# Q and K of 128 later rows computed during the weight load, kept in DRAM, and read back in steps 16 to 19, with a new order and ungated last loads

## The chip, the cores and the metric

The kernel runs on one core of one Trainium2 chip. The metric is device time in microseconds, the median of the runs shown. Before the change it is 2654.93 us (three runs, 2654.26 to 2665.12).

## The reference

A transformer of two layers with one set of weights, over 2048 rows `x` of width 576, bfloat16. Each layer is a memory-augmented attention and a gated feed-forward, both on a layer norm of the residual stream:

```python
for s in range(n_seg):                       # 64 segments of 32 rows
    xs = x[:, s * seg_len:(s + 1) * seg_len, :]
    h = concatenate([mem, xs], axis=1)       # 8 memory rows + 32 rows
    q, k, v = h @ Wq, h @ Wk, h @ Wv         # 32 heads of 128
    p = softmax(where(mask, q @ k.T * scale, -1e9))
    o = (p @ v) @ Wo
    mem = o[:, :M, :]                        # memory of the next segment
    outs.append(o[:, M:, :])
...
x = x + A(layernorm(x)); x = x + B(layernorm(x))     # B: (silu(x w1) * (x w3)) w2, F = 4608
x = x + A(layernorm(x)); x = x + B(layernorm(x))
```

The memory makes the segments a chain: segment s+1 needs the eight memory rows that segment s puts out. Q and K of the 32 rows of a segment don't need the memory.

## The kernel before

**Steps.** The two layers run interleaved. In step t, layer 0 treats segment t and layer 1 segment t - 8 (`LAG`, line 32), so there are 72 steps. Steps 0 to 7 and 64 to 71 treat one layer, those between both, and then the matmuls for Q and K read 80 columns (twice 8 memory rows and 32 rows), otherwise 40. `role(t)` (line 58) is the parity; the columns lie in the tile HT, 160 + 16 of them per pair of steps, so that the odd step starts at column 96 (`qcols`, line 960). A step works in four groups of eight heads (line 27). For each group it does Q and K (`qk`, line 969; `qk_tail`, 987, for the last 64 of the 576 rows of the weights, Q and K on one half of the array's rows each), evicts them to a slot of QKT (`qk_ev`, 1001; four slots, line 42), computes scores, softmax on VectorE and ScalarE, transposes the probabilities PB to PTS (in two-layer steps by a DMA transpose on the SP queue, `ptr_dma`, 1098), multiplies with V (`pv`), evicts to OT and projects with WO (`wo`, `wo_tail`). At the end of the step the memory rows go back into HT (`y_mem`, 1175), after ScalarE copied the upper half of the last 64 output rows to YO (`y_odd`, 1169); the other rows go to YTS (`yts`, 1203), from where, every four steps, `post_tr` (1216) transposes them for the residual sum.

**The feed-forward** fills the gaps: one job per four steps (`job`, 487), each with 18 pairs of 256 columns of w1, w3 and w2, which are loaded anew for every job into two slots each of W13 and W2C through SP. HTT holds its middle values.

**The start.** All attention weights are loaded first (lines 276 to 281), 19 MB through SP and ScalarE's queue, by groups of eight heads of Wq and Wk, then Wv in part, then Wo in four parts. Step 0 can only proceed as these land. In step 0, `qk` also issues 12 matmuls of 512 columns on the identity for a unit whose full part comes before its tail (lines 976 to 978), whose results aren't used.

**The end.** When the attention weights have been read for the last time, the weights of the last feed-forward are loaded over them (`tail_load`, 775): for each of eight parts, w1 and w3 into W, w2 into WV. From part 1 on, a load also waits for a gate: part 1 for the output projection of group 1 of the last step, parts 2 to 7 for that of group 3 (line 572; the wait is set at line 788 and stands on SP).

**The order.** `make_nodes` (248) makes a node for each piece of work with an engine, a duration, dependencies and a priority; `plan` (94) simulates the engines and gives each node its place. TensorE's order isn't found there: it is the string `ORDER` (line 238), one letter per node (line 90: Q and q for QK and its tail, S scores, P times V, O and o the projection, F and f the feed-forward's first part, W and w its second). The other engines' queues, SP's too, and the buffer slots follow from the estimated durations. A change of TensorE's tiling mode between nodes is priced in `SWITCHES` (line 38). The instructions are recorded in the planned order by helpers, so that nearly all have the same few lines: L659 is every matmul, L662 ScalarE, L665 VectorE, L668 a DMA on SP, L1103 the transposes.

Of the kernel before, what the change touches and what calls it, by code (L numbers as in the profile page):

```python
# [13 lines left out]
P = 128  # L14
# [19 lines left out]
PTR = 112  # L34

# [7 lines left out]
         "xr": 3, "xn": 2, "w13": 2, "w2": 2, "htt": 4}  # L43
# [46 lines left out]
KINDS = {"m0tr": "m", "L0tr": "a", "L1tr": "b", "POST": "p", "Ftr": "n", "QK": "Q", "QKt": "q", "SC": "S", "TR": "T", "PV": "P",  # L90
# [121 lines left out]
def ewh(*ns):  # L212
# [5 lines left out]
    "maQqSQQvqqVSxXTqSPQSTOPXoTPOTPoOoOoQqqQvSSqVqQSQTPSTOPOToPToxPOOooQqqQSqvSaVQQSqTPSTPOOoTPoTPOOooQqqQSQSvqVQTSqX"  # L218
    "SPTPOTOPoToxPOOooQqqpQvSSVqnQfFSTFfqQPWSTOPFTOfPFTofoPOOooWQFfqqfFSQQSqqfFvVfTFSPQWTSFPXffOTFPOTOPWOooooaxQqqQSW"
    "FSQvfqTVfSFPQFTfqOPSWTOPFOTffoooPFOoWQqqvSQQSFfqVfSTWqFQFSPTfPOTWPoTOPOOooobQpvVqqqQQSnQqfxFSXqqfFQQQPSWFqqfQOfS"  # L220
    "PFxXoFPfOWOofPFOooFQqqfWQQSqqqQQQSFfqgfFGSQPQqgqfGOSPFWGgfOoPFoGgfWOPFOooFQqqfqQWSQQvqVSFffqFQQqqPQSqWQPSfFOFOPW"
    "OafFPofooOoWQQqqqqQSQQbSqqqQGSgQqPQGggSPGGPgOOOPoooOoQqqvpQpQQnSqqVqnSQFffqFQQPQqqfSFSfFOPWwOooFPffFOWPwOooFqqfq"
    "QQQSFqqfqQQQSWwGSFqqfgQQPwWgSGFPGgfOOPWgfGFPOOooooFaqqfQQQQqqwSSVvQQqqfFWFSPwqfqQQPFSwfOWOFPffFOwPWOooooFfqqqQQW"
    "SQQqqqQSbQGSgqqQPQGSgOPGggOPGwOPoooOo"
)
FOUR = (
    "QqqqqQppQQvVSSnnQFfqqQFqSfQQPFfqOwPoSWFffOPFWOowoPFOoFffqqQQQQqqWSwFSGgfqqQQQPQqqgWSSGFPFffggGGPwOFOPOOffooowoFv"
    "VqqqQQQWSFqfqqQQQSwWFPSFfqqfQQPwOSWFFPoffOOWPwOoooFfqqQQWaSqqQQQbSQqgqGSQPQqqgGSOPoGggOPGwOPooOo"
# [4 lines left out]
    "QPFSTOPofFTOPwTWPOOoooFfqfqQQSQSFvqfVfqFTQPSWwSTFPxXffTFPOOTWOPwOFooooFqffqQQSWwVvqfSQFfqTQPSWTwPOSFOTfFPwTOPWOo"  # L233
    "oooFqfqfFQQWSfqSFwvVQQTSqffPWwSTFFPOoTOWPoTwPOOoobQpqxqvVSnQXqfFSQTQSPFfqOoTSFfPTwPOOoofTFPFOowQfqqQSQSFvqfVTqfF"
    "PQTSwPSXffFTOOPwTOPFOooooFxqfQQqqSvVSQTQSFPfqfOTSPwoOTFPFTOPoofOowQQfqqFSSvVqQQSqTwPTSPOOFTofPTPOOooopfffFFFnwfw"
    "FFffFFwfFffFwffwFFFFffwFwfffFFFwffFFwfffFFww"
)
ORDER = FIRST + FOUR * 11 + LAST
# [9 lines left out]
def make_nodes(em, nseg, pools, o=Opt, dma_bw=230e3, load_bw=345e3):  # L248
# [24 lines left out]
    def load(name, nbytes, prio, fn, deps=()):  # L273
        return node("DMA", nbytes / load_bw, fn, deps=deps, prio=prio, name=name, lat=2.0)

    ld_m0 = node("ACT", 0.1, em.load_m0(), prio=-90, name="m0", lat=2.5)
    ld_t = [load("ldt", kb(3 * R64, 4096), -10.0, em.load_tails(0)), node("ACT", 0.1, em.load_tails(1), prio=-120, name="ldt", lat=6.0)]
    node("ACT", 0.1, em.load_tails(2), prio=-80, name="ldt", lat=6.0)
# [3 lines left out]

    b = banks(1)
# [10 lines left out]
    def ln_nodes(tag, src, xn, deps, prio, writes, warm=False):  # L294
# [5 lines left out]
        d = node("PE", 5 * 0.056, em.ln_tr(xn, b, warm), deps=[c], prio=prio, mode="col", acq=[b], rel=[xn], name=tag + "tr")  # L300
# [5 lines left out]
    def ht_writes(li, g):  # L306

        out, at = [], {}
        for j in range(4):
            at.setdefault((4 * g + j - role(4 * g + j + LAG * li)), []).append(j)  # L310
        for te, js in at.items():
            te += LAG * li - R_HT
            cost = ewh(240, 80, 80) if li and both(te + R_HT) else ewh(160 * len(js))
            out.append(((lambda js: lambda b: em.ht_write(li, g, js, b))(js), cost, reads_ht.get(te, []) + reads_ht.get(te + 1, [])))
        return out
# [9 lines left out]
    vx_ev, last_v, pvs = {}, [], {}  # L325

    def v_nodes(name, t, k, prio, tail_at, emit, strips, deps, tail_deps, free):
# [3 lines left out]
        m_ = node("PE", 8 * 0.2158 + 0.11, emit(b, False), deps=deps, prio=prio, mode=modes[0], acq=b, name=name)  # L331
        n = node("PE", 0.2158, emit(b, True), deps=deps + tail_deps, prio=prio + tail_at, mode=modes[1], acq=b, name=name + "t")
# [39 lines left out]
    def step(t):  # L372
# [6 lines left out]
        mm80 = max(c80 / 2.4 + 2.5, 25.0) / 1000  # L379
        rd = reads_ht.setdefault(t, [])  # L380

# [9 lines left out]
        for g, (h0, nh) in enumerate(GROUPS):  # L391
            qs, qe = [], []
            for uh, un in units(g, nl):
# [3 lines left out]
                m_ = node("PE", 8 * un * mm80, em.qk(t, uh, un, b), deps=hx + hm[:1] + ([ld_h[g]] if t == 0 else []),  # L397
                          prio=pq, mode="full", acq=[q] + b, name="QK")
                n = node("PE", un * mm80, em.qk_tail(t, uh, un, b), deps=hx + hm + ([ld_h[g]] if t == 0 else []), prio=pq + o.qkt, mode="row",
# [3 lines left out]
                for r in (0, 1):  # L403
                    cost = ew(un * 64, un * 16) if e == 0 else ew(un * 48, un * 32)
                    qe.append(node("AD", cost if nl == 2 else ew(un * 40), em.qk_ev(t, un, r, q, b[r]), deps=[m_, n], prio=t + o.ustep * uh / 4,
                                   rel=[b[r]], name="QKe"))
# [5 lines left out]
            sc = node("PE", nh * (0.0165 * nl if nl == 2 else 0.0255), em.scores(t, g, qs, s), deps=qe, prio=pf + o.sc, mode="col" if nl == 2 else "full/col",  # L412
# [5 lines left out]
            d = node("DVE", dve(w40) + 0.2, em.sm_sum(t, g, sme), deps=[c], prio=pf, name="sum")  # L418
            w = 0.168 * (4 - e if nl == 2 else 2) + nl * w40 / 960
            pbs = node("DVE", w, em.sm_pb(t, g, sme, pb), deps=[d], prio=pf, acq=[pb], rel=[sme], name="pb")  # L420
            pts = Slot("pts")
            if nl == 2:
                tr = node("DMA", 1.27 * nh / 8, em.ptr_dma(t, g, pb, pts), deps=[pbs], prio=pf - 0.02, acq=[pts], name="TR", lat=2.45)
# [25 lines left out]
            wot = node("PE", nh / 2 * mm80, em.wo_tail(t, g, ot), deps=[wo], prio=t + o.wo + o.wog * h0 / 8, mode="col", rel=[ot], name="WOt")  # L449
# [30 lines left out]
    last_up = []  # L480
# [6 lines left out]
    def job(j):  # L487
# [24 lines left out]
        def units(pps, at0, end):  # L512
            for at, pp in enumerate(pps, at0):
# [3 lines left out]
                for pr_ in (2 * pp, 2 * pp + 1):  # L517
# [8 lines left out]
                    else:  # L526
# [3 lines left out]
                        ld = [node("DMA", kb(1152, 256) / dma_bw, em.load_w13(pr_, w13), prio=prio - 1, acq=[w13], lat=2.8, name="W13")]  # L530
                        lds.append(node("DMA", kb(256, 576) / dma_bw, em.load_w2(pr_, w2), prio=prio - 0.99, acq=[w2], lat=2.0, name="W2l"))
# [6 lines left out]
                    ff = node("PE", 2 * mm, em.ffn_up(ents, pr_, w13, b, in_tail, True), deps=wr + ld, prio=prio + o.fft, mode="row",  # L538
                              acq=b + [htt], rel=rel13, name="FFt")
                    a = node("ACT", actc(256 * ne), em.ffn_tanh(ents, b, htt), deps=[fm, ff], prio=prio - 0.5, name="tanh")  # L540
                    c = node("DVE", 2 * dve(256 * ne) + 0.13, em.ffn_mul(ents, b, htt), deps=[a], prio=prio - 0.5, rel=b, name="mul")
# [27 lines left out]
        if last:  # L569
            v_done, qk_done = last_reads  # L570
            me = steps[nst - 1]
            gates = {1: me["WO1"], **{i: me[f"WO{NG - 1}"] for i in range(2, 8)}}
            for i in range(8):
                g = gates.get(i)
                tail.append([load("tail", kb(128, c), s0 + o.tail_at + 0.01 * i, em.tail_load(i, what, g), deps=dep + [g])
# [18 lines left out]
    def x_in(g):  # L594
        xn = Slot("xn")
        ld = node("DMA" if g else "ACT", 0.8 if g else 0.1, em.load_xn(g, xn), deps=reads_ht.get(4 * g - 3, [])[:1], prio=4 * g - 3.0 if g else -100, acq=[xn],
                  name="ldxn", lat=2.5)
        ht_set(0, g, ln_nodes("L0", xn, xn, [ld], 4 * g - 2.0 if g else -8, ht_writes(0, g)))
        xr[g] = Slot("xr")

# [7 lines left out]
    ht_mem[0] = [node("DVE", 0.1, em.init_mem(0, 0), deps=[m0e], prio=-4, name="m0")]  # L608
    for t in range(nst):
# [25 lines left out]
class Emitter:  # L635
# [119 lines left out]
    def load_xn(self, g, xn):  # L755
        return lambda n: (self.dma if g else self.adma)(self.T.XN[:, xn.i, :], self.a.x[g * P:(g + 1) * P, :])
# [107 lines left out]
    def ht_write(self, li, g, js, b):  # L864

        def f(n):
# [15 lines left out]
            if k:  # L882
# [3 lines left out]
                cp(80, 40, 16)  # L886
            else:
# [76 lines left out]

    def nl(self, t):
# [3 lines left out]
    def qk(self, t, uh, un, b):  # L969

        def f(n):
            q0, q1 = self.qcols(t)
            w = q1 - q0
# [463 lines left out]
```

## Time and profile before

| what | value |
|---|---|
| median of the runs shown | 2654.93 us |
| the profiled execution's own time | 2657.81 us |
| its span | 2656.0 us |
| mean granted TensorE clock | 0.992 |
| TensorE busy | 2578.3 us (97%) |
| VectorE busy | 2004.1 us (75%) |
| ScalarE busy | 1242.3 us (47%) |
| matmuls of Q and K, HT and W | 23040, 785.1 us |
| moved by DMA | 371.48 MB, 140 GB/s |

The span is what the profiler saw of the program; the time of the same execution is 1.8 us longer. Busy times are unions, and weight loads (PEld) run beside matmuls. In the slices each digit is the busy share of a fortieth of the span, 66.4 us. In the windows each engine's busy time in a stretch is followed by its number of instructions, then come the granted clock (1.00 is full rate), the busy share of the DMA engines and GB/s. In the timeline, the columns are the start, the duration of a run of like instructions, engine, line, operation, what it writes and reads, shape and number.

### The profile page before, as it was taken

The numbers are of one execution on the slowest core, as the hardware profiler recorded it, in microseconds if no ns is written. First come the engines' busy times: TensorE is split into PE (matmuls) and PEld (weight loads), VectorE is DVE, ScalarE is ACT, GpSimd is POOL, SyncE is SP. The second block draws the span as 40 slices with busy tenths as digits, with TensorE's granted clock in tenths as the row PEclk, the third lists the DMA queues.
The fourth block names the chain that finished last, engine by engine and source line by source line (L and its number), as shares of the span: only waits on it lengthen the run. The fifth ranks groups of instructions, "written<-read, shape, count | busy, mean of one in ns | idle before, by whom it ended". The sixth has DMA issues, their size and how long they took to land.

```text
span 2656.0 us, 133410 instructions
## 1 busy us (share of the span) xinstructions
PE 2578.3 (97%) x59426; PEld 2216.6 (83%) x59426; DVE 2004.1 (75%) x5137; ACT 1242.3 (47%) x3495; POOL 335.2 (13%) x399
## 2 busy tenths in 40 slices
PE   6899999999999999999999999999999999999998
PEld 4788878888888888888888888888888888888887
DVE  4677777877787778778777877877787787777866
ACT  2555453444545444454544544454444445454443
POOL 1111111110101111010101101110110111011110
PEclk8899999999999999999999999999999999999999
DMA  9055746556554655555465555645565554554458
GB/s 322 4 153 150 182 101 152 128 131 157 117 141 108 152 135 126 155 128 139 109 143 134 138 146 125 146 106 151 122 147 139 132 140 106 129 139 131 130 155 244
DMA packets 690433, 371.48 MB, mean 140 GB/s; under 512 B 234328, under 2 KB 682592, under 8 KB 689216
## 3 DMA queue, kind: packets, MB, share of 16 engines
q1 hardware_dynamic: 686320, 355.08, 53.5%
q8 instruction: 464, 7.60, 1.2%
q0 software_dynamic: 3024, 6.93, 0.9%
q10 hardware_dynamic: 512, 0.94, 0.2%
q14 instruction: 113, 0.93, 0.1%
HBM read 306.72 MB, written 2.36 MB: 116 GB/s over the span
## 4 chain that ended last, share of the span: by engine, by line
PE 83%; DMA 9%; DVE 5%; ACT 1%; issue 1%; SPq 1%; POOL 0%; ACTq 0%; DVEq 0%; POOLq 0%
PE bank L659 83%; DMA PTS<-PB 5%; DMA W<-in_B_w_dram 1%; DMA W2C<-in_B_w_dram 1%; DVE STAT L665 1%; DMA WV<-in_A_Wv_dram 1%; DVE SME L665 1%; DVE PB L665 1%; SPq L668 1%; DVE V L665 0%; DMA W<-in_A_Wq_dram 0%; ACT V L662 0%; DVE XR L665 0%; DVE HTT L665 0%; DVE LNS L665 0%
## 5 line engine op out<-in xcount | busy, mean ns | idle before, releaser
L659 PEld LDWEIGHTS <-W 128*128 128x128 bf16 (+2 forms) x32464 | 1259.9, 100 | 118.1 <-issue 63.6
L659 PE MATMUL bank<-HT,W 128*128 128x80 bf16 (+3 forms) x23040 | 785.1, 197 | 16.1 <-issue 9.3
L659 PE MATMUL bank<-XTB,W 128*64 128x256 bf16 (+5 forms) x9424 | 658.9, 263 | 2.0 <-DMA W<-in_B_w_dram 2.0
L1093 POOL MEMSET PB<- 128x1024 bf16 x288 | 273.9, 951 | 1944.4 <-DMA PTS<-PB 1142.8
L662 ACT ACTIVATE QKT<-bank 128x256 bf16<-128x256 f32 (+4 forms) x1423 | 342.4, 320 | 246.4 <-PE bank L659 216.9
L659 PE MATMUL bank<-OT,WO 128*128 128x80 bf16 (+3 forms) x11520 | 421.2, 199 | 1.0 <-ACT OT L662 0.5
L662 ACT ACTIVATE V<-bank 64x512 bf16<-64x512 f32 (+1 forms) x605 | 339.6, 585 | 164.9 <-PE bank L659 158.4
L659 PEld LDWEIGHTS <-WO 128*128 128x128 bf16 (+1 forms) x11520 | 387.8, 102 | 34.0 <-issue 18.7
L659 PE MATMUL bank<-WV,HT 128*32 128x512 bf16 (+4 forms) x3768 | 370.4, 386 | 5.1 <-DMA WV<-in_A_Wv_dram 4.5
L659 PE MATMUL bank<-W2C,HTT 128*64 128x288 bf16 (+1 forms) x3216 | 321.8, 287 | 3.4 <-DMA W2C<-in_B_w_dram 2.8
L662 ACT ACTIVATE OT<-bank 128x320 bf16<-128x320 f32 x374 | 153.8, 437 | 313.2 <-PE bank L659 309.3
L665 DVE TENSOR_REDUCE STAT<-SME 104x8 f32<-104x320 f32 (+1 forms) x576 | 275.1, 478 | 27.9 <-ACT SME L662 22.3
L665 DVE TENSOR_TENSOR PB<-SME,STAT 40x128 bf16<-40x128 f32 (+4 forms) x912 | 275.4, 336 | 12.1 <-DVE STAT L665 0.4
L665 DVE SCALAR_TENSOR_TENSOR HTT<-HTT,bank 128x512 bf16<-128x512 bf16 (+1 forms) x324 | 201.5, 622 | 106.7 <-ACT HTT L662 103.7
L659 PEld LDWEIGHTS <-HT 128*32 128x32 bf16 (+4 forms) x3768 | 155.4, 100 | 145.2 <-issue 39.1
L659 PEld LDWEIGHTS <-HTT 128*64 128x64 bf16 (+1 forms) x3288 | 230.1, 105 | 40.8 <-issue 7.3
L662 ACT ACTIVATE HTT<-bank 128x512 bf16<-128x512 f32 (+1 forms) x324 | 173.9, 548 | 179.9 <-PE bank L659 178.3
L665 DVE SCALAR_TENSOR_TENSOR XR<-bank,XR 128x288 f32<-128x288 f32 x574 | 241.5, 447 | 14.4 <-PE bank L659 11.0
L662 ACT ACTIVATE SME<-SME 104x320 f32<-104x320 f32 (+1 forms) x288 | 135.1, 469 | 241.4 <-DVE SME L665 238.1
L665 DVE TENSOR_TENSOR HTT<-HTT,bank 128x512 bf16<-128x512 bf16 (+1 forms) x324 | 203.7, 629 | 33.0 <-PE bank L659 0.5
L665 DVE CAST QKT<-bank 128x192 bf16<-128x192 f32 (+2 forms) x497 | 141.4, 328 | 104.7 <-PE bank L659 102.5
L665 DVE CAST V<-bank 64x512 bf16<-64x512 f32 (+1 forms) x259 | 177.3, 684 | 36.9 <-PE bank L659 33.0
(60 smaller groups left out, 1394.4 us busy)
## 6 DMA issues: line engine op xcount, KB each, us to landing
W<-in_B_w_dram SPq DMA_DIRECT2D x608, 256.0 KB, 3.9
W2C<-in_B_w_dram SPq DMA_DIRECT2D x304, 288.0 KB, 3.5
W<-in_B_w_dram SPq DMA_DIRECT2D x608, 32.0 KB, 3.9
W<-in_B_w_dram SPq DMA_DIRECT2D x16, 512.0 KB, 8.3
WO<-in_A_Wo_dram SPq DMA_DIRECT2D x4, 1152.0 KB, 10.0
XR<-in_A_x_dram POOLq DMA_DIRECT2D x16, 288.0 KB, 4.0
WV<-in_B_w_dram SPq DMA_DIRECT2D x8, 576.0 KB, 7.3
W<-in_A_Wq_dram SPq DMA_DIRECT2D x16, 256.0 KB, 5.8
```

The lines of the kernel that those rows point to most:

```text
L659: self.ch("PE", self.nc.tensor.matmul(out, lhsT=lhsT, rhs=rhs, start=start, stop=stop, skip_group_check=True, **k))
L662: self.ch("ACT", self.nc.scalar.activation(*a, **k))
L665: self.ch("DVE", getattr(self.nc.vector, fn_)(*a, **k))
L668: self.ch("SP", self.nc.sync.dma_start(out=out, in_=in_))
L1093: return lambda n: self.ch("POOL", self.nc.gpsimd.memset(self.T.PB[:, pb.i, 0:GROUPS[g][1]], 0.0))
```

## The change

`PRE = (4,)` names the fifth group of 128 rows of `x`, the rows that layer 0 treats in steps 16 to 19. A new function `ahead` makes nodes for it: load the rows, layer norm, transpose into one half of XTB, then for eight units of four heads compute Q and K of all 128 rows (letters K and k), evict them into a stage of 128 x 1024 (the stages lie in W13, W2C and HTT, which aren't in use yet) and store them to a DRAM tile XQ. The letters K and k stand in the order's part for step 0.

In steps 16 to 19, `qk` and `qk_tail` read only 48 columns: the 40 of layer 1 and the 8 memory rows of layer 0. In the even step these are two runs of 24 columns. `xq_load` fetches the other 32 columns per head and kind from XQ straight into the slot of QKT, 32 loads in all, on SP. `qk_ev` then copies 40 and 8 columns instead of 64 and 16 or 48 and 32. HT gets 8 more columns, into which `ht_write` copies 8 columns once more.

The tail chunks of YTS of the two layers now share one column block, which makes room. The loads of the last feed-forward have no gates (`GATES = {}`). Several durations and latencies in `make_nodes` are changed, and the first feed-forward loads depend on the stores. `FIRST`, `FOUR` and `LAST` are new strings; `FIRST` covers four steps more, and `FOUR` is repeated ten times, not eleven.

```diff
+PRE = (4,)
+AHEAD = True
+BACK = 4
+GATES = {}
...
-         "xr": 3, "xn": 2, "w13": 2, "w2": 2, "htt": 4}
+         "xr": 3, "xn": 2, "w13": 2, "w2": 2, "htt": 4, "stage": 8}
...
-    "maQqSQQvqqVSxXTqSPQSTOPXoTPOTPoOoOoQqqQvSSqVqQSQTPSTOPOToPToxPOOooQqqQSqvSaVQQSqTPSTPOOoTPoTPOOooQqqQSQSvqVQTSqX"
+    "mcaKKQQqkSKkqTkQqkkKSSKKkvXxxVXqQPTKPSTOKoPOTOooPkOokQqQSqqqSQQvSSTVPTPTOPOTOPoooOoQqqQSqvSVQQSqTPSTPOOTPTooPOOo"
...
-ORDER = FIRST + FOUR * 11 + LAST
+ORDER = FIRST + FOUR * 10 + LAST
...
-def make_nodes(em, nseg, pools, o=Opt, dma_bw=230e3, load_bw=345e3):
+def make_nodes(em, nseg, pools, o=Opt, dma_bw=230e3, load_bw=380e3, tail_bw=330e3):
...
+        pre = t // 4 in PRE and both(t)
+        mmq = max((48 if pre else c80) / 2.4 + 2.7, 25.1) / 1000
...
+                xl = []
+                if pre:
+                    xl.append(node("DMA", 1.0, em.xq_load(t, uh, q), deps=[v[0] for v in [kept_qk.get((t // 4, uh // 4))] if v] + last_qk[-BACK:][:1], prio=pq - 0.3, acq=[q], lat=2.3, name="XL"))
...
-            gates = {1: me["WO1"], **{i: me[f"WO{NG - 1}"] for i in range(2, 8)}}
+            gates = {i: me[k] for i, k in GATES.items()}
...
+    def ahead(i, g):
+
+        half = 1 - i % 2
+        xn = Slot("xn")
+        ld = node("DMA" if i else "ACT", 0.8 if i else 0.1, em.load_xn(g, xn), deps=kept_qk[g_[i - 1], 0][1:] if i else [], prio=-2.5 if i else -95, acq=[xn],
+                  name="ldxn", lat=3.1 if i else 9.6)
...
+        for u in range(H // 4):
+            b = banks()
+            st = Slot("stage")
+            w = ld_h[group_of(u)]
+            m_ = node("PE", 32 * (P / 2.4 + 2.5) / 1000, em.xq(half, u, b, False), deps=wr + [w], prio=prio + 0.5 * u, mode="full/col", acq=b + [st], name="XQ")
+            n = node("PE", 4 * (P / 2.4 + 2.5) / 1000, em.xq(half, u, b, True), deps=wr + [w], prio=prio + 0.5 * u, mode="row", acq=b + [st], name="XQt")
+            es = [node("AD", ew(512), em.xq_ev(r, b[r], st), deps=[m_, n], prio=prio + 0.5 * u + 8, rel=[b[r]], name="XQe") for r in (0, 1)]
+            kept_qk[g, u] = [node("DMA", kb(P, 1024) / 300e3, em.xq_store(i, u, st), deps=es, prio=0.1 + i + 0.01 * u, rel=[st], lat=2.0, name="XQs")] + [n]
...
+        if role(t):
+            return H_[rows, c, q0 + 40:q0 + 88], 48
+        x = H_[rows, c, q0 + 56:q0 + 80]
+        return bass.AP(x.tensor, x.offset, [list(v) for v in x.ap][:1] + [[-56, 2], [1, 24]]), 48
...
+    def xq_load(self, t, uh, q):
+
+        def f(n):
+            at = QW if role(t) else MEM
+            o = self.T.QKT[:, q.i, 0:8 * SW].rearrange("p (b n) -> p b n", n=SW)[:, :, at:at + SEG]
+            self.dma(o, self.T.XQ[PRE.index(t // 4), uh // 4][:, t % 4 * 256:(t % 4 + 1) * 256].rearrange("p (b n) -> p b n", n=SEG))
+        return f
...
+                for d0, s0, m in ((40, 0, 40), (0, 40, 8)) if role(t) == 0 else ((0, 8, 40), (72, 0, 8)):
+                    self.cp(n, dst[:, :, d0:d0 + m], src[:, :, s0:s0 + m])
...
-    T.HT = sp.tile([P, R_HT // 2, 5, 2 * SW + 2 * MEM], BF, name="HT")
+    T.HT = sp.tile([P, R_HT // 2, 5, 2 * SW + 3 * MEM], BF, name="HT")
...
-    T.YTS = sp.tile([P, 2, 5, P], BF, name="YTS")
+    T.YTS = sp.tile([P, 9, P], BF, name="YTS")
```

## The prediction on record

> **What bounds the kernel now.** I read the page first: shares of busy time, then the slices.
>
> ```profile
> span 2656.0 us, 133410 instructions
> PE 2578.3 (97%) x59426; PEld 2216.6 (83%) x59426; DVE 2004.1 (75%) x5137; ACT 1242.3 (47%) x3495; POOL 335.2 (13%) x399
> ...
> PE   6899999999999999999999999999999999999998
> ...
> PEclk8899999999999999999999999999999999999999
> DMA  9055746556554655555465555645565554554458
> ```
>
> TensorE is busy 97% of the span, and only the first two slices (66 us each) lie below 9. Almost everywhere the sum of its work sets the time; at the start the DMA row (9, then 0) says that loads do. A change must therefore take work off TensorE, or fit added work into the start. Next the windows of the four steps that the change treats; a step ends with the copy into YO.
>
> ```profile
> core 0: us, PE busy (x) PEld busy (x) DVE busy (x) ACT busy (x) POOL busy (x), PEclk, DMA share, GB/s
> 532.80:571.70 38.90, 38.90 (x863) 34.23 (x861) 30.28 (x78) 18.77 (x55) 5.18 (x6) 1.00 0.61 143
> 571.70:614.50 42.80, 42.15 (x890) 36.48 (x886) 31.49 (x79) 19.10 (x54) 4.35 (x5) 1.00 0.57 132
> 614.50:655.10 40.60, 40.12 (x930) 35.97 (x926) 32.46 (x83) 16.05 (x49) 3.81 (x4) 1.00 0.68 157
> 655.10:688.10 33.00, 31.81 (x709) 25.73 (x706) 23.84 (x65) 18.96 (x57) 5.47 (x7) 1.00 0.46 96
> ```
>
> Steps 16 to 19 last 155.3 us, TensorE idles 2.3 us of it, and VectorE, the next, is busy 118.1 us. DMA is busy .61 x 38.9 + .57 x 42.8 + .68 x 40.6 + .46 x 33.0 = 90.9 us.
>
> **Part by part.** All sums are against the profiled execution: span 2656.0, its time 2657.8, while the median shown is 2654.9; I carry differences over to the median.
>
> *Narrower Q and K in steps 16 to 19.* Each step issues 256 full matmuls and 64 tails, the tails two at a time on half the rows each: 288 slots. What a slot costs comes from the timeline of TensorE, uninterrupted runs of 64:
>
> ```profile
> 71.30 1.75 PE L659 MATMUL bank<-HT,W 128*128 128x40 bf16 x64
> ...
> 536.22 2.46 PE L659 MATMUL bank<-HT,W 128*128 128x80 bf16 x64
> ```
>
> One matmul shows .18 (40 columns) or .20 us (80), so the pitch is (1.75 - .18) / 63 = 24.9 ns and (2.46 - .20) / 63 = 35.9 ns. No row has 48 columns. The lower end is the 40-column 24.9, the upper the straight line between the rows, 27.1; I take 24.9, the nearer row. Saving 4 x 288 x 11.0 ns = **-12.7 us**; at 27.1 it is 10.1. If a right side in two runs of 24 cost as much as 80 columns, 0; the probabilities also reach TensorE in two runs (lines by form: PTS,V with 80 columns, mean 202 ns, as HT,W), so I exclude that. [...]
>
> *The same work at the start.* Eight units of 36 slots of 128 columns; the end of the kernel has such a run, 72 in 4.17 us, (4.17 - .22) / 71 = 55.6 ns. 8 x 36 x 55.6 = 16.0 us, plus ten transposes of the layer norm (.7 us, row at 12.22) and some twelve mode switches at the planner's .1: 17.9 us. What can hide it:
>
> ```profile
> 21.00:28.00 7.00, 5.77 (x97) 3.65 (x91) 3.16 (x8) 0.91 (x2) 0.00 (x0) 1.00 1.05 402
> 28.00:35.00 7.00, 5.28 (x128) 3.29 (x127) 0.89 (x2) 0.77 (x2) 0.00 (x0) 1.00 1.01 421
> 35.00:42.00 7.00, 4.23 (x48) 1.36 (x51) 2.00 (x4) 1.85 (x4) 0.00 (x0) 0.56 1.03 384
> 42.00:49.00 7.00, 4.96 (x128) 3.70 (x120) 6.67 (x15) 4.85 (x10) 0.96 (x1) 0.74 1.07 374
> 49.00:56.00 7.00, 5.92 (x147) 4.21 (x148) 4.03 (x12) 2.76 (x7) 1.90 (x2) 0.72 1.11 379
> ```
>
> From 14 us (first weights) to 61 (end of step 0) TensorE idles 9.9 of 47 us. The clock column .56, .74, .72 means 2 x (.44 + .26 + .28) x 7 = 13.7 us at half rate, up to 6.9 us of work lost; they follow the idle stretches, which the new matmuls fill. I leave 2 us idle: 17.9 - 7.9 - 6.9 = 3.1, and .4 for 144 KB more to load ahead of the weights: **+3.5 us** on the path, since step 0 ends with the output projection, whose weights land last. Bounds: 0 (all fits) and 17.9 (nothing does). The 16 evictions of 512 columns (.6 us each by the V rows, 9.6 in sum) lie on VectorE and ScalarE, busy 17 and 14 of these 47 us; uncovered they would delay step 0's softmax by a microsecond or two. The eight stores (2.1 MB, 6 us at 375 GB/s) stand on SP ahead of the next x load and the first feed-forward weights, and the DMA row is nearly 0 from 61 to 139 us; nothing waits.
>
> *Loads of the kept part.* 32 loads of 64 KB in pieces of 64 bytes, so 1024 packets, 64 per DMA engine, each issued on SP once a QKT slot is free. Behind a load that waits stand the transposes of the probabilities and weight loads. The trace has no 64-byte packet. In its packet records the semaphore packets of 4 bytes took 9 ns and the 256-byte ones of the transposes 18 (median); the mean over the busiest queue is 53.5% x 2656 x 16 / 686320 = 33. I take 18, the nearest size: 2048 x 18 = 37 us, DMA busy 128 of 142.6 us instead of 91 of 155. A load then lands after about the 3.1 us of a transpose; between two scores that use one slot lie some 9 us of TensorE. The transposes, whose landings cost TensorE 1.5 us in these steps, queue behind: I take **+2.0 us**, bounds 0 and 16 x 1.2 = 19.
>
> ```profile
> q1 hardware_dynamic: 686320, 355.08, 53.5%
> ...
> PTS<-PB SPq DMA_TRANSPOSE x224, 3.1
> ```
>
> The evictions of Q and K shrink (128x256 and 128x64 to 128x160 and 128x32), off the path: 0. The added copy of 8 columns into HT, the shared tail column of YTS (a wait behind five transposes of .47 us) and the new tile sizes: 0, as VectorE and ScalarE have slack; a few tenths if not.
>
> *No gates at the end.*
>
> ```profile
> 2597.00:2607.00 10.00, 7.66 (x222) 6.68 (x218) 5.95 (x18) 5.95 (x14) 1.90 (x2) 0.83 0.38 109
> 2607.00:2615.00 8.00, 6.52 (x211) 5.92 (x207) 3.92 (x13) 2.93 (x8) 1.90 (x2) 1.00 0.80 239
> 2615.00:2646.00 31.00, 31.00 (x520) 26.17 (x517) 23.09 (x58) 8.06 (x20) 1.13 (x2) 1.00 1.09 335
> ```
>
> DMA is at .38 while gates hold the last weights, then full, and TensorE waits 1.0 us for W at 2648. Ungated, the loads end 6 to 8 us sooner; TensorE, busy throughout, is late next. **-1.5 us**, bounds -4 and +1.
>
> *New order.* Counted by the planner's own rule, a group of four has 66 mode switches instead of 65 (ten groups, +1.0 us at .095), the end 217 instead of 224 (-.7): **+.3**. TensorE's idle time is 77.7 us; without the start (22.8) and steps 16 to 19 some 52 are left. Durations nearer to the measured ones should save a little: **-2.0**, bounds +8 and -15, as no view of before shows the new order.
>
> Sum: -12.7 + 3.5 + 2.0 - 1.5 + .3 - 2.0 = -10.4. On the profiled time 2647.4, on the median **2644.5 us**.
>
> **Rivals.**
> A, the sum above: 2644.5, its own range 2637 to 2651, chance .46.
> B, the order is worth more. From 61 to 130 us the clock columns are .93, .78, .85 for 23, 24 and 22 us: 20 us at half rate, up to 10 lost. If half of that goes, and 7 us more of the idle time: 2632. For: these steps have little else to run. Against: ten groups of four have about 1.3 us idle each, so little can be won there. Chance .28.
> C, the start isn't covered: idle stretches remain because chains, not a lack of work, make them (softmax of the last heads), and 17.9 is paid nearly in full: 2655 to 2659, no change. For: TensorE waits 3.1 us for PTS there. Chance .17.
> D, on the other side: the scratch loads make DMA the bound in steps 16 to 19. At the mean of 33 ns a packet DMA needs 90.9 + 67.6 = 158.5 us, longer than 155.3, and transposes come late: 2658. From 31 ns the kernel is slower than before, from 38 measurably; at 45 ns 2683. Against: a third of the packets took far less than the mean. Chance .09. [...]
>
> That narrower matmuls save nothing is within C.
>
> **The numbers.** A measurement of this kernel can tell about 0.5%, 13.3 us: faster is below 2641.7, slower above 2668.2. B and a quarter of A are faster: .40. The rest of A, C and a part of D: .53. Slower: .07, most of D. The range 2628 to 2661 leaves out the lower part of B and the upper of D.
>
> **What would show it.** Runs of 128x48 at 25 ns a slot and steps 16 to 19 near 145 us; step 0's YO copy at 62 to 66 us instead of 60.6, with the clock at 1.0 between 35 and 56; DMA share near .9 in steps 16 to 19, without scores waiting for QKT; no low DMA share before the end. I am wrong if step 0 ends after 70, if PTS or scratch loads end waits of TensorE for over 5 us, or if the groups of four differ from 153.5 us by over 0.7 each.

## The result, and the profile after

| | median of six runs, us | range |
|---|---|---|
| before | 2655.32 | 2653.78 to 2665.12 |
| after | 2671.21 | 2670.77 to 2674.73 |

The ratio is 1.0057, with a 95% interval of 1.0043 to 1.0071: the changed kernel is slower by 0.6%. The forecast was 2644.5 us, and its range ended at 2661. So the prediction was wrong in sign and in size. All times that are compared here are of executions at a granted clock of .97 or more; one of no_warm, a run below, had .707 and 3299.96 us and is not counted.

The first lines and the slices of the page of after (profiled execution 2670.77 us):

```profile
span 2669.0 us, 133559 instructions
PE 2576.8 (97%) x59379; PEld 2217.2 (83%) x59436; DVE 2037.2 (76%) x5178; ACT 1224.3 (46%) x3478; POOL 335.9 (13%) x400
...
PE   7899999999999999999999999999999999999988
...
PEclk9899999999999999999999999999999999999999
DMA  9154846578554656555455555645565564554457
```

TensorE's busy time has hardly changed (2578.3 before, 2576.8 now), and the span is 13 us longer: most of the loss is waiting. The busy time of after is a little too low, though: the page has 59379 matmuls (PE) for 59436 weight loads (PEld), so 57 matmuls left no record and count as idle time. The slices can't show where, since a digit hides up to 6.6 us. So the span is cut at the ends of steps (the copy into YO), the same way in each kernel. The first number of a cell is the stage's length, the second TensorE's idle time in it, both in us.

| kernel | 0 | 1–7 | 8–15 | 16–19 | 20–59 | 60–71 | rest | span |
|---|---|---|---|---|---|---|---|---|
| before | 60.6/22.8 | 176.9/14.7 | 295.2/7.7 | 155.3/2.3 | 1539.1/13.5 | 386.4/11.6 | 42.4 | 2656.0 |
| after | 66.5/17.1 | 172.2/13.8 | 299.5/10.0 | 148.8/5.5 | 1548.7/24.3 | 391.0/17.1 | 42.2 | 2669.0 |
| difference in length | +5.9 | -4.7 | +4.3 | -6.5 | +9.6 | +4.6 | -0.2 | +13.0 |

The four treated steps gain 6.5 us, the start costs 1.2 net by the end of step 7, and 14.2 us are lost in steps 20 to 71, whose work the change leaves alone (the new letters only split some of it differently into halves of the array, which is why the number of matmuls differs below). How far a single profile can be trusted: in eight kernels of this study whose program is the same there, steps 8 to 15 took 292.9 to 299.5 us, so a stage is known to some 3 us, and the 4.3 us of steps 8 to 15 are no finding.

The treated steps by window, in after:

```profile
core 0: us, PE busy (x) PEld busy (x) DVE busy (x) ACT busy (x) POOL busy (x), PEclk, DMA share, GB/s
538.30:572.10 33.80, 33.08 (x812) 28.20 (x808) 29.38 (x73) 17.16 (x56) 4.92 (x6) 1.00 0.70 129
572.10:617.40 45.30, 43.83 (x920) 36.95 (x923) 34.28 (x85) 18.33 (x55) 4.36 (x5) 1.00 0.83 186
617.40:656.90 39.50, 38.85 (x892) 33.31 (x888) 30.48 (x74) 16.48 (x54) 3.81 (x4) 1.00 0.78 161
656.90:687.00 30.10, 27.42 (x645) 20.72 (x644) 23.33 (x61) 16.72 (x59) 5.43 (x7) 1.00 0.58 108
```

The step bounds shift against each other, so the sum counts. TensorE's busy time falls from 153.0 to 143.2 us, by 9.8, and its idle time rises by 3.2 (about 1 us of both is five matmuls without a record). DMA is busy .70 x 33.8 + .83 x 45.3 + .78 x 39.5 + .58 x 30.1 = 109.5 us, 18.6 more than before, where I had added 37.

The narrow matmuls, in the timeline of TensorE in after:

```profile
550.45 0.96 PE L703 MATMUL bank<-HT,W 128*128 128x48 bf16 x32
```

One takes .183 us (median), so the pitch is (.96 - .183) / 31 = 25.1 ns: what the 40-column row had given. All matmuls of Q and K over 128 rows in steps 16 to 19, before and after, with busy time and mean ns of one:

```profile
L659 PE MATMUL bank<-HT,W 128*128 128x80 bf16 x1030 | 40.0, 202 | 0.3 <-ACT HT L662 0.3
```

```profile
L703 PE MATMUL bank<-HT,W 128*128 128x48 bf16 x1022 | 29.3, 183 | 0.0
```

With the tails (7.5 and 7.0 us) and .4 of six matmuls of the next step that reach into the window of after, Q and K fall from 47.5 to 36.7 us, so 10.8 of the 12.7 us arrived.

The DMA issues of after, with count, KB and the median from issue to landing:

```profile
PTS<-PB SPq DMA_TRANSPOSE x224, 3.1
...
QKT<-XQ SPq DMA_DIRECT2D x32, 64.0 KB, 3.2
```

A scratch load lands 3.2 us after its issue. Its 64-byte packets took 11 ns in the packet records (median of 32768), not the 18 I took.

The start, in after, windows as before:

```profile
35.00:42.00 7.00, 6.95 (x149) 5.40 (x146) 1.18 (x2) 1.42 (x4) 0.91 (x1) 1.00 1.03 391
42.00:49.00 7.00, 7.00 (x145) 5.09 (x142) 5.54 (x16) 3.47 (x8) 0.00 (x0) 1.00 1.06 373
49.00:56.00 7.00, 6.58 (x177) 4.45 (x170) 6.36 (x10) 5.39 (x10) 0.87 (x1) 1.00 1.08 388
56.00:61.00 5.00, 4.53 (x111) 4.46 (x110) 2.02 (x5) 1.31 (x3) 1.03 (x2) 1.00 0.66 250
...
84.00:108.00 24.00, 20.63 (x691) 18.55 (x687) 19.48 (x52) 14.42 (x33) 5.24 (x6) 0.86 0.02 4
108.00:130.00 22.00, 20.49 (x692) 17.00 (x690) 13.39 (x39) 12.46 (x31) 4.55 (x6) 0.96 0.02 4
```

The new work does fill the idle time, and the clock column is 1.00 where it was .56, .74 and .72. DMA is full to 56 us, and the last piece of WO lands at 56.6 (56.4 before). Yet it is not this landing that makes step 0 end 5.9 us later. The output projections, before (up to 80 us, so with those of step 1) and after, with min/median/max in ns and first and last start:

```profile
L659 PE MATMUL bank<-OT,WO x239: 179/180/208, 50.0 to 80.0; 128*128 128x40 bf16 x96, 128*64 128x40 bf16 x24
```

```profile
L703 PE MATMUL bank<-OT,WO x160: 179/179/207, 58.4 to 65.9; 128*128 128x40 bf16 x128, 128*64 128x40 bf16 x32
```

Before, they began at 50.0 us, as the pieces of WO came; now the first begins at 58.4, when all of WO is there. The chain of work that ended last, from 40 us to the end of step 0 in after, is TensorE's own work:

```profile
by line: PE bank L703 94.5%; issue 3.9%; ACT OT L706 1.7%
```

Before, it was so for 66% of the time from 40 to 61 us, the rest being mostly the evictions of V and the softmax. Between 84 and 130 us the clock is .86 and .96 instead of .78 and .85: part of the 4.7 us that steps 1 to 7 give back.

Steps 20 to 59 as one window, before and then after:

```profile
688.10:2227.20 1539.10, 1525.56 (x33704) 1322.68 (x33701) 1180.00 (x3020) 728.47 (x2130) 187.97 (x220) 1.00 0.55 134
```

```profile
687.00:2235.80 1548.80, 1524.49 (x33347) 1321.87 (x33384) 1203.19 (x3040) 712.97 (x2111) 188.30 (x220) 1.00 0.56 134
```

In the window of after, matmuls fall short of the weight loads by 37 (x33347, x33384). Gates_back, a run described below whose program is the same in these steps, has all records:

```profile
684.30:2232.10 1547.80, 1528.22 (x33386) 1322.14 (x33384) 1203.06 (x3040) 712.97 (x2111) 188.12 (x220) 1.00 0.56 134
```

There the loss against before is 8.7 us, of which 6.0 are waiting and 2.7 busy time. In the five kernels with this program the steps took 1547.2 to 1549.2 us. VectorE has 23 us more work and ScalarE 15.5 less: of 320 evictions of OT, 90 were on VectorE before and 130 are now, of 480 of V 140 and 150, because `plan` decides it from the estimated durations. The waits of TensorE in these steps, total us, times and the longest, before and after:

```profile
PE bank L659 <- DMA PTS<-PB: 9.9, 16, 0.9
PE bank L659 <- ACT HT L662: 3.4, 10, 0.3
```

```profile
PE bank L703 <- DMA PTS<-PB: 12.1, 18, 1.3
PE bank L703 <- ACT HT L706: 3.8, 11, 0.3
PE bank L703 <- issue: 3.2, 20, 0.2
PE bank L703 <- DVE V L709: 1.7, 7, 0.5
PE bank L703 <- DMA W<-in_B_w_dram: 1.3, 2, 1.1
```

The twenty gaps of "issue" (no cause in the profile) are not there in gates_back; they go with the missing records. No single wait took the loss; there are 2.2 us more for the transposed probabilities, and small ones on V and W.

### The profile page after: what moved, and what is told of

Read it like the earlier page. It is cut to its first block, busy times and chain, and to the rows that moved or that the text cites. A ratio compares the mean times of both kernels' runs of the same rounds, so it can differ in the third digit from the quotient of the medians.

```text
span 2669.0 us, 133559 instructions
## 1 busy us (share of the span) xinstructions
PE 2576.8 (97%) x59379; PEld 2217.2 (83%) x59436; DVE 2037.2 (76%) x5178; ACT 1224.3 (46%) x3478; POOL 335.9 (13%) x400
## 4 chain that ended last, share of the span: by engine, by line
PE 76%; DVE 12%; DMA 8%; issue 2%; ACT 1%; SPq 1%; POOL 0%; ACTq 0%; DVEq 0%; POOLq 0%
PE bank L703 76%; DMA PTS<-PB 5%; DVE STAT L709 2%; DVE SME L709 2%; DVE HTT L709 2%; DVE PB L709 2%; DVE V L709 1%; DMA W2C<-in_B_w_dram 1%; DVE QKT L709 1%; DMA W<-in_B_w_dram 1%; DVE XR L709 1%; DVE LNS L709 1%; SPq L712 0%; DVE OT L709 0%; DMA WV<-in_A_Wv_dram 0%
## 5 line engine op out<-in xcount | busy, mean ns | idle before, releaser
L703 PE MATMUL bank<-HT,W 128*128 128x80 bf16 (+4 forms) x23040 | 779.2, 196 | 17.7 <-issue 10.8
L703 PE MATMUL bank<-XTB,W 128*64 128x256 bf16 (+5 forms) x9648 | 683.6, 262 | 9.2 <-issue 5.4
L706 ACT ACTIVATE QKT<-bank 128x256 bf16<-128x256 f32 (+6 forms) x1466 | 341.7, 312 | 284.9 <-PE bank L703 269.3
L703 PE MATMUL bank<-OT,WO 128*128 128x80 bf16 (+3 forms) x11520 | 410.2, 198 | 2.2 <-issue 1.9
L703 PEld LDWEIGHTS <-WO 128*128 128x128 bf16 (+1 forms) x11520 | 382.5, 102 | 30.2 <-issue 15.1
L703 PE MATMUL bank<-WV,HT 128*32 128x512 bf16 (+4 forms) x3610 | 360.6, 382 | 6.7 <-issue 4.5
L706 ACT ACTIVATE OT<-bank 128x320 bf16<-128x320 f32 x324 | 136.7, 437 | 321.7 <-PE bank L703 317.7
L709 DVE TENSOR_TENSOR PB<-SME,STAT 40x128 bf16<-40x128 f32 (+4 forms) x912 | 275.2, 336 | 11.6 <-DVE STAT L709 0.4
L703 PEld LDWEIGHTS <-HT 128*32 128x32 bf16 (+5 forms) x3664 | 155.4, 99 | 137.7 <-issue 33.7
L703 PEld LDWEIGHTS <-HTT 128*128 128x128 bf16 (+1 forms) x3192 | 229.8, 105 | 44.2 <-issue 6.7
L709 DVE CAST QKT<-bank 128x192 bf16<-128x192 f32 (+3 forms) x454 | 129.5, 328 | 104.9 <-PE bank L703 102.1
L709 DVE CAST V<-bank 64x512 bf16<-64x512 f32 (+1 forms) x268 | 183.8, 686 | 20.7 <-PE bank L703 15.3
```

Of the source, the lines that this page charges most:

```text
L703: self.ch("PE", self.nc.tensor.matmul(out, lhsT=lhsT, rhs=rhs, start=start, stop=stop, skip_group_check=True, **k))
L706: self.ch("ACT", self.nc.scalar.activation(*a, **k))
L709: self.ch("DVE", getattr(self.nc.vector, fn_)(*a, **k))
```

## The experiments

The theory with which they began: the loss is the new order, that is, TensorE's string together with the durations from which the other engines' queues are planned. Its rivals: the scratch loads, the start, and one single duration. All ratios below are to the kernel before on the same chip. The stages are those of one profiled execution each.

### The letters and the durations, one by one and both

Where `NEW` and `OLD` are the whole strings; steps 0 and 1 keep their new letters:

```diff
 old_letters
-ORDER = FIRST + FOUR * 10 + LAST
+ORDER = NEW[:91] + OLD[74:]
 old_durations (all durations shared with the kernel before; some of them)
-load_bw=380e3, tail_bw=330e3
+load_bw=345e3, tail_bw=345e3
-            w = (1.04 - 0.07 * e if nl == 2 else 0.46) * nh / 8
+            w = 0.168 * (4 - e if nl == 2 else 2) + nl * w40 / 960
-            sc = node("PE", nh * (0.0155 * nl if nl == 2 else 0.0255), ...
+            sc = node("PE", nh * (0.0165 * nl if nl == 2 else 0.0255), ...
 old_both: both edits
```

> The changed kernel, but with the order string of before from step 2 on (the new string stands for steps 0 and 1 alone); durations as changed. Theory L, the new letters cost the time: steps 20 to 59 fall from 1548.7 back to about 1539 us and steps 60 to 71 from 391.0 to about 386.5, while steps 8 to 15, whose letters are the same in both strings, stay at 299.5; total about 2657 us. Theory D, the changed durations cost it, because they set the queues of the other engines: steps 20 to 59 stay near 1548, total 2668 to 2674. Theory S, the changed tiles and queues of the code cost it: 2668 to 2674 as well.

> The changed kernel with its own letters, but every duration, latency and load rate that both versions have is set back to that of before. Theory D: steps 8 to 15 fall from 299.5 to about 295 us, steps 20 to 59 from 1548.7 to about 1540, total about 2653 us. Theory L: steps 20 to 59 stay at 1548 and the total is at 2666 to 2671 us. Theory S: nothing changes, 2671 us.

> Old letters from step 2 on and old durations together: what is left is the change's own work (start, scratch loads, narrow matmuls, tiles, no gates). Theories L and D both give steps 8 to 15 at 295, 20 to 59 at 1539, 60 to 71 at 386 us, and 2671 - 4.3 - 9.6 - 4.6 = 2652 to 2653 us. Theory S: 2668 to 2672 us, with steps 20 to 59 still at 1548.

| kernel | median, ratio | 16–19 | 20–59 | 60–71 |
|---|---|---|---|---|
| old_letters | 2692.85, 1.0161 (1.0140 to 1.0183) | 161.8/15.4 | 1556.9/22.3 | 389.2/15.7 |
| old_durations | 2673.14, 1.0084 (1.0058 to 1.0110) | 151.4/6.2 | 1542.9/15.3 | 391.5/16.2 |
| old_both | 2677.20, 1.0106 (1.0079 to 1.0133) | 160.1/12.6 | 1540.6/13.6 | 388.6/13.2 |

In steps 20 to 59 the four pairs stand thus: old letters with old durations 1540.6, new letters with old durations 1542.9, new with new 1548.7, old letters with new durations 1556.9. Profiles of kernels whose program is the same there differ by 2 us (the five with the new pair) to 5 us (three kernels below). So the 2 us that the new letters cost with the old durations are within the spread, the 6 us that the new durations cost with the new letters are barely beyond it, and the 16 us that they cost with the old letters are clear of it. This points to the durations more than to the letters. That a string suits the durations beside which it was found shows with the new durations alone, where the new letters are 8 us better.

The forecasts of the totals missed for all three kernels: 2657 (theory L), 2653 (theory D) and 2652 to 2653 us. Old_durations is in the median no faster than after (1.0084 and 1.0057), although its steps 20 to 59 are 6 us shorter in the profile. Its profiled execution, 2668.08 us, is the fastest of four that reach to 2678.72, and that of old_both, 2672.53, the fastest of four to 2682.39; where the slower ones lose, no trace shows.

In steps 16 to 19 it is the letters that count: with the old ones TensorE idles 15.4 and 12.6 us, and the narrower matmuls bring nothing. So the new string is needed there.

The window of 20 to 59 in old_durations shows the other engines going back with the durations:

```profile
690.10:2232.90 1542.80, 1527.55 (x33384) 1321.48 (x33381) 1191.77 (x3030) 722.99 (x2120) 188.72 (x220) 1.00 0.56 134
```

VectorE's 1191.8 us lie between 1180.0 and 1203.2.

### One duration alone: that of PB

```diff
 old_pb
-            w = (1.04 - 0.07 * e if nl == 2 else 0.46) * nh / 8
+            w = 0.168 * (4 - e if nl == 2 else 2) + nl * w40 / 960
 old_but_pb: all other shared durations old, this one new
```

> The changed kernel with a single duration set back, that of writing the probabilities PB (1.04 and 0.97 us to 1.34 and 1.17; a run of its four instructions took 1.12 us). Theory P: the shorter duration gives VectorE less time in the plan than it needs, so the plan moves evictions to it and the softmax falls behind. Then VectorE's share of the OT evictions in steps 20 to 59 falls from 130 to about 90 of 320, these steps from 1548.7 to about 1543 us, total 2663 to 2666. Theory Q, the sum of the other durations does it: steps 20 to 59 stay at 1547 to 1549, total 2670 to 2674.

> The counterpart: all shared durations of before but that of PB, which stays as changed. Theory P: steps 20 to 59 stay near 1549 us with about 130 evictions of OT on VectorE. Theory Q: they fall to about 1543 us with 90, total 2666 to 2673.

Old_but_pb took 2687.55 us, 1.0130 (1.0106 to 1.0154), with 1549.3 us in steps 20 to 59. There theory P held: beside the otherwise old durations, the new one of PB alone takes these steps from 1542.9 to 1549.3 us, about as much as all the new durations together cost with these letters, and the evictions of OT on VectorE from 90 to 130. Each is one profile, and the 6 us are little more than the spread. The window:

```profile
701.10:2250.40 1549.30, 1529.87 (x33386) 1322.61 (x33383) 1212.28 (x3090) 707.51 (x2060) 187.81 (x220) 1.00 0.55 133
```

That the moved evictions make the loss isn't shown, as no run moves them alone.

Old_pb took 2748.18 us, 1.0358 (1.0332 to 1.0385), with 1617.9 us in steps 20 to 59 and 120 evictions of OT on VectorE. Here theory P failed: beside the other new durations the old one of PB repairs nothing, old_pb is 80 us worse than after ((1.0358 - 1.0057) x 2655). The window, and the first line of TensorE's waits in it:

```profile
692.50:2310.40 1617.90, 1548.48 (x33386) 1338.89 (x33383) 1213.62 (x3080) 701.43 (x2071) 188.98 (x220) 0.98 0.52 128
```

```profile
PE bank L703 <- DMA PTS<-PB: 62.8, 29, 5.7
```

What makes them is seen in its timeline, all engines; "x4" is the number of like instructions, and the bracket is the idle time before and what ended it:

```profile
717.13 1.12 DVE L709 TENSOR_TENSOR PB<-SME,STAT 40x128 bf16<-40x128 f32 x4
...
719.39 2.30 SPq L712 DMA_DIRECT2D W<-in_B_w_dram  x4
721.79 6.88 SPq L1211 DMA_TRANSPOSE PTS<-PB  x2
725.27 0.71 PE L703 MATMUL bank<-PTS,V 128*128 128x80 bf16 x8 [4.79 <-DMA PTS<-PB]
```

PB is written by 718.25, but its transpose is issued at 721.79, behind weight loads that stand ahead of it on SP and wait for a slot (from 712 to 727 us, four waits of SP on TensorE's matmuls, 3.6 us in all, the longest 2.2). The durations for PB are 1.34 and 1.17 us in old_pb, 1.04 and .97 in after; beside the other new durations the longer ones make the plan believe the probabilities later than they are, and it puts the loads ahead. TensorE stood for 4.8 us. The trace has such a wait, of 4.5 to 5.7 us, once in each of the ten groups of four. Against gates_back these steps have 50 us more of idle time (69.4 and 19.6) and 20 us more of busy time: around each of the ten waits the clock is granted at half for 3.4 to 6.9 us.

### The scratch loads

```diff
 no_loads (the slot keeps what it held: Q and K of those 32 columns are left out in steps 16 to 19)
-            self.dma(o, self.T.XQ[PRE.index(t // 4), uh // 4]...
+            o if True else self.dma(o, self.T.XQ[PRE.index(t // 4), uh // 4]...
```

> The changed kernel without the 32 loads of the kept Q and K in steps 16 to 19 (the slots keep old contents there); everything else is the same. Theory X, the loads and the transposes behind them cost what is missing of the 12.7 us: steps 16 to 19 fall from 148.8 to 143 to 144 us, idle from 5.5 to under 2, total 2664 to 2666. Theory L, the order of these steps costs it: they stay at 147 to 149 us, total 2669 to 2672.

Median 2668.83, 1.0061 (1.0038 to 1.0084); steps 16 to 19 took 148.0 us against 148.8 in after. TensorE's waits in these steps, in after and then without the loads:

```profile
PE bank L703 <- DMA PTS<-PB: 2.2, 3, 1.5
```

```profile
PE bank L703 <- DMA PTS<-PB: 2.6, 2, 1.6
```

The .8 us are within the spread: seven kernels with these loads and the same program in these steps (after, gates_back, no_warm, late_k and the three of the last experiment) took 146.0 to 149.2 us. The transposes cost TensorE no less without the loads. The loads are not the cause.

### The start: without the unused matmuls, and with less new work in step 0

Both kernels, before and after, issue 36 matmuls in step 0 whose results are not used:

```diff
 no_warm
-            for c in range(4 if first and t == 0 else 0):
+            for c in range(0):
 late_k (two units K, k of the new work leave step 0)
-    "...XqQPTKPSTOKoPOTOooPkOokQqQSqqqSQQvSSTVPTPTOPOTOPoooOo..."
+    "...XqQPTPSTOoPOTOooPOoQqQSqqqSQQvSSTVPTPTKkOPOTKkOPoooOo..."
```

> The changed kernel without the 36 matmuls on the identity in step 0, whose results nothing reads (7.7 us at full clock). Theory W, step 0 is bound by TensorE's work now: its YO copy comes at 59 to 61 us instead of 66.6, total 2664 to 2666 us. Theory C, step 0 is bound by the landing of WO and by the softmax chain: YO stays at 65 to 67 us, total 2671 us, or some us more if the clock falls to half rate between 20 and 60 us as it did before.

> The changed kernel with the last two of the eight units of kept Q and K (4 us of TensorE) moved from step 0 into waits of step 1. Theory W, from 42 us on (Wv landed) step 0 is bound by TensorE's work: the YO copy of step 0 comes at 62 to 63 us instead of 66.5, and steps 1 to 7 grow by less, as they hold 13.8 us of idle time; total 2 to 4 us less, 2667 to 2669. Theory C, step 0 is bound by WO's landing and the softmax chain: YO stays at 65 to 67 us, and steps 1 to 7 grow by up to 4; total 2671 to 2675.

No_warm: median 2657.93, 1.0026 (1.0013 to 1.0038). Late_k: 2665.34, 1.0061 (1.0044 to 1.0078). Windows of the start, of no_warm and then of late_k:

```profile
28.00:35.00 7.00, 4.73 (x146) 4.20 (x145) 3.27 (x8) 2.81 (x6) 0.96 (x1) 0.92 1.01 418
35.00:42.00 7.00, 5.87 (x84) 5.41 (x79) 1.66 (x4) 1.03 (x2) 0.00 (x0) 0.59 1.02 391
```

```profile
56.00:61.00 5.00, 3.66 (x119) 3.38 (x115) 2.29 (x6) 2.21 (x6) 1.90 (x2) 0.81 0.64 240
61.00:67.50 6.50, 4.45 (x126) 4.23 (x124) 1.21 (x4) 1.23 (x4) 0.95 (x1) 0.50 0.01 3
```

Without the 36 matmuls step 0 is 1.8 us shorter, no more: TensorE idles from 28 to 35, and a stretch at half rate (.59) follows. With work taken out of step 0, step 0 is not shorter but 1.0 us longer (67.5), since TensorE idles after 56 us and runs at half rate (.50) to 67.5, just where the output projection ends the step. So the 5.9 us of step 0 are not simply added work; that reading fell. The work, the idle time and the clock trade against each other, and steps 0 to 7 together stay at 237.5 to 241.1 us in before, after, no_warm, no_loads, gates_back and late_k. That no_warm is 8 us better than after by the ratios (.0031 x 2655) is not explained by the start: its steps 0 to 7 are .7 us longer than those of after, and its gain lies in 8 to 15 (5.4 us, a stretch at half rate, 240.7 to 244.1 us in after, that is gone), 60 to 71 and elsewhere, in steps whose program is the same. Why is open.

### The gates

```diff
 gates_back
-GATES = {}
+GATES = {1: "WO1", **{i: "WO3" for i in range(2, 8)}}
```

> The changed kernel with the gates of before on the last loads. Theory G, loads without gates crowd the DMA queue while the last steps still need other loads: steps 60 to 71 fall from 391.0 to 387 or 388 us, the tail stays at 42 us, total 2667 to 2668. Theory N, the gates decide nothing, as TensorE's work bounds the tail: both stay within 0.5 us, or the tail grows by the 1.0 us that TensorE waited for W before; total 2670 to 2673.

Median 2665.73, 1.0052 (1.0032 to 1.0072). Steps 60 to 71 took 387.4 us (391.0 without gates), what follows them 44.6 (42.2). TensorE's wait on the last weights, with gates:

```profile
PE bank L703 <- DMA W<-in_B_w_dram: 1.6, 1, 1.6
```

In after there is no such wait, as forecast. More can't be told. Behind step 71 the four kernels without gates and with this program (after, no_loads, no_warm, late_k) took 42.0 to 43.2 us, the five with gates (before, gates_back and the three below) 41.9 to 44.8; steps 60 to 71 took 387.6 to 393.7 without gates, and the 387.4 of gates_back lie at their lower end.

### The new pair to step 19, the old pair from step 20

```diff
 halves (each duration shared with the kernel before: new to step 19, old from step 20; gates back)
-ORDER = FIRST + FOUR * 10 + LAST
+ORDER = NEW[:934] + OLD[917:]
-        d = node("PE", 5 * 0.06, em.ln_tr(xn, b, warm), ...
+        d = node("PE", 5 * c_(0.06, 0.056), em.ln_tr(xn, b, warm), ...
 halves_no_warm: halves without the 36 unused matmuls
 halves_late_k: halves_no_warm with the start of late_k
```

> The changed kernel with its new letters and durations only up to step 19; from step 20 on the letters and the durations of before, and the gates of before at the end. Theory M: what was lost from step 20 on belongs to the new letters and durations as a pair; then steps 20 to 59 last 1540 to 1543 us instead of 1548, steps 60 to 71 386 to 388 instead of 391, and the total is 2655 to 2660 us. Theory S, the changed tiles or queues cost it: 1547 to 1550 us and a total of 2666 to 2671.

> halves, also without the 36 unused matmuls of step 0. If what no_warm won (13 us in the median, 1.8 of them in step 0, 4 in step 8 with the half-rate stretch at 241 us gone) comes again: 2643 to 2648 us. If it was the place of that one stretch: the 2 us of step 0 alone, 2652 to 2657.

> halves_no_warm, also with the two units in step 1. By theory W and theory M together: step 0 at 61 us, steps 16 to 19 at 148, steps 20 to 59 at 1541, total 2645 to 2651 us, so 0.1 to 0.3% under before. If theory W is wrong: as halves_no_warm or 2 us more.

| kernel | median, ratio | 0 | 1–7 | 8–15 | 16–19 | 20–59 | 60–71 |
|---|---|---|---|---|---|---|---|
| halves | 2651.96, 1.0011 (0.9999 to 1.0024) | 66.4/16.4 | 171.5/13.3 | 295.6/5.8 | 148.9/3.9 | 1544.7/17.1 | 382.6/10.6 |
| halves_no_warm | 2645.36, 0.9984 (0.9974 to 0.9994) | 64.4/19.7 | 174.6/15.1 | 292.9/5.4 | 146.0/2.3 | 1539.8/12.2 | 382.7/9.3 |
| halves_late_k | 2643.40, 0.9977 (0.9964 to 0.9989) | 63.8/22.6 | 173.9/12.3 | 294.0/6.6 | 146.1/2.3 | 1539.7/12.6 | 379.8/8.1 |

The pair from step 20 on is what made the kernel slower. Halves differs from gates_back in this pair alone, and the ratio falls from 1.0052 (1.0032 to 1.0072) to 1.0011, 11 us, while the saving in steps 16 to 19 stays. Steps 20 to 59 take 1539.7 to 1544.7 us in the three kernels, 1547.2 to 1549.2 in the five with the new pair; halves itself missed its 1540 to 1543. The window of 20 to 59 of halves_no_warm is that of before again:

```profile
677.80:2217.70 1539.90, 1527.73 (x33707) 1322.73 (x33705) 1188.41 (x3030) 730.17 (x2121) 188.01 (x220) 1.00 0.55 134
```

Halves_late_k is the fastest kernel of the study, 0.2% below the kernel before; that late_k's letters themselves help isn't shown, as the two intervals overlap. Nor is it shown that the change itself gains. Halves, which has the 36 unused matmuls as before has them, is level with before (0.9999 to 1.0024). The 7 us from there to halves_no_warm come with leaving them out, 4.9 of them in steps 20 to 59, where the program is the same; the kernel before was not run without them.

## Why the prediction was wrong

| term | forecast | measured |
|---|---|---|
| narrower Q and K | -12.7 | pitch 25.1 ns, as taken; -10.8 in the rows of Q and K |
| scratch loads | +2.0 | +.8, within the spread |
| steps 16 to 19 as a whole | -10.7 | -6.5 (-6.1 to -9.3 in seven kernels) |
| start | +3.5 | +1.2 (steps 0 to 7) |
| no gates | -1.5 | nothing clear of the spread |
| new order | -1.7, bounds +8 and -15 | 8–15 +4.3, 20–59 +9.6, 60–71 +4.6: +18.5 |

**The step that failed is "New order".** I took its mode switches as known (+.3) and guessed that durations nearer to the measured ones would save 2 us. The sum of the last row is 20 us off and lies outside its bounds. It holds chance in steps 8 to 15, and "issue" gaps in steps 60 to 71 (see below); 20 to 59 alone, +9.6, is outside too. The reason I gave was wrong. PB's new duration is nearer to the measured 1.12 us than the old one (1.04 and 1.34), and yet beside the old others these steps took 6 us more with it, by one profile each: what a changed duration does is replan the queues of the other engines, for better or worse. Halves shows that the old pair takes the loss away. The mode switches were a small error beside it: counted by `plan`, a group of four has 66 in both strings and the end 202 instead of 206, so the +.3 should have been -.4 at the planner's price, which no run measures. My test for being wrong, groups of four that differ by more than .7 us, was met: (1548.7 - 1539.1) / 10 = .96.

**Steps 16 to 19.** The pitch was right, and yet 4.2 us are missing in after. In the rows of Q and K 10.8 of the 12.7 us arrived. The new letters of these four steps hold 86 mode switches by `plan` where the old held 66, 20 x .095 = 1.9 us, while the prediction counted none here; that price is the planner's, and no run measures it. The 3.2 us of added idle time are partly chance: the seven kernels with this program have 2.3 to 5.5 us.

**Start.** The size was within its bounds, and the new work does fill the idle stretches and keep the clock at 1.0. What ends step 0 I had wrong: not the landing of WO but TensorE's own work, 94.5% of the chain from 40 us on. I looked only at step 0, where the cost is 5.9; the steps behind it give back 4.7.

**The rivals.** Rival A is the forecast. B needed a gain from the order, and the order lost; of its other half, the half-rate stretches up to about 130 us, a part came (20.6 us before, 13.7 in after). C, a start that isn't covered, would have shown in steps 0 to 7. D, the only one on the slower side, didn't happen: at 11 ns a packet DMA is busy 109.5 of 148.8 us, and without the loads the steps are .8 us shorter. The time came out near D's for another reason, which no rival of mine held: that a replanned order loses in the steps that the change doesn't treat.

**What TensorE waits for in "issue".** In steps 60 to 71 most of the added idle time has this name: 13.1 us in after, 8.0 before. The page of after has a queue whose packets go with these gaps, with packets, MB and share of the DMA time:

```profile
q8 instruction: 465, 7.62, 1.2%
```

These 465 packets of 16384 bytes stand against 118815 matmuls and weight loads, one for every 256. In before and the twelve runs of the experiments, whose traces have a record for every matmul, I counted matmuls and weight loads ahead of every "issue" gap of over .4 us, 188 in all: the counts differ by multiples of 256, and each gap ends 1.2 to 1.7 us behind the end of such a packet. I read this as TensorE waiting for its next instructions, from these counts and times alone; no view names such a wait. In steps 60 to 71 the gaps took 8.0 us before, 9.0 in old_both and 4.2 to 5.1 in the three halves kernels, all with the old letters and durations there, and 9.4 to 13.6 in the five kernels with the new pair. They vary as much among kernels with one pair as between the pairs, so part of the 4.6 us of steps 60 to 71 can't be put down to the order.

**What stays open.** Whether and how PB's new duration costs some 6 us in steps 20 to 59, why the "issue" gaps come where they do, and why leaving out 36 matmuls at the start gains 7 to 8 us in steps whose program is the same.

## What to carry to other kernels

An engine's order and the estimated durations that plan the other queues are one thing: a truer estimate replans these queues, and the pair has to be timed again on the chip, stage by stage, before any gain is credited to it. When a change replans everything, keep the old plan for the stages that it doesn't treat; here that was worth 11 us, nearly as much as the change itself could save. Count what the plan prices in an order, mode switches too, by the stage in which it stands, and follow a cost at the start for some steps: here steps 1 to 7 gave back 4.7 of the 5.9 us.

## What was unexpected of the hardware

- A packet of 64 bytes took 11 ns (median). A load of 64 KB in 1024 such packets landed 3.2 us after its issue, as soon as a transpose of the probabilities (3.1), and 32 of them cost nothing clear of the spread, with DMA at .58 to .83.
- Before, TensorE was granted half the clock from 97.3 to 111.0 us, although in the 18.8 us ahead of that it was busy 17.1 and no gap was over .91 us; from 61 to 78.5 us it was busy 14.1 of 17.5 at the full clock. The stretches move when work is moved: 35.9 to 42.7 and 46.1 to 53.0 us before, none of these in after, 33.9 to 40.7 in no_warm, 59.1 to 69.3 in late_k. With two units of work taken out, step 0 took 67.5 us in late_k, against 66.5 in after.
- One of the planner's constants, longer by .2 to .3 us, was worth 80 us, since weight loads that waited for their slots held up the transposes behind them on SP (4.5 to 5.7 us, ten times), with stretches at half rate around them (3.4 to 6.9 us each).
- TensorE had "issue" gaps of up to 3.3 us (old_both); those of over .4 us stood a multiple of 256 matmuls and weight loads apart, in before and all twelve runs.
